# Output product of a gated feed-forward kernel: seven smaller products in place of a full product, taken product by product

## The chip, the cores and the metric

The kernel runs on one core of a Trainium2 chip. The metric is the device time of one execution in microseconds (us). A difference below about 0.3% cannot be told from no change here.

## The reference

Attention within chunks of 64 tokens, then a gated feed-forward layer over 4608 tokens with 512 features, all in fp32.

```python
# batch 8, heads 8, seq 576, head_dim 64, chunks of 64
scores = scale * (q_c @ k_c.T); attn = softmax(scores); out = attn @ v_c
x = out.transpose(0, 2, 1, 3).reshape(4608, 512)
xn = x / sqrt(mean(x * x, -1) + 1e-06) * rms_g
g = xn @ w_gate                       # w_gate, w_val: 512 x 1536
val = xn @ w_val
return (g * sigmoid(g) * val) @ w_out # w_out: 1536 x 512
```

## The kernel before

Every fp32 matrix is split into a high and a low part (`h`, `l`), and a product is three matmuls: high by high, high by low, low by high. All large matmuls have 128 columns of weights and 512 moving elements.

The tokens are nine tiles of 512 (`TT`). The first three tiles (tile zero, one, two; the loop `for t in range(PLAIN)`) take both layers as plain products: `gated` makes one 128-wide slice of the hidden features and `down` adds its share of the output to four PSUM banks `acc`. While tile zero runs, the weights are converted (`conv_step`); while tile one runs, the weights' sums for the gating products are made on GpSimd and stored to DRAM (`sides`, `save_plain`).

The last six tiles are three **blocks** of two tiles each (`for b in range(NB)`). In a block the gating product is taken in seven products instead of eight, by the scheme of Strassen and Winograd: tokens of the two tiles, and halves of the feature sums, are combined, and `product` takes one of the seven, P1 to P7, for one pair `i` of hidden slices (`up_pair`, six pairs per block). In each pair the order is P1, P5, P6, P2, P3, P7, P4 (`ORD`; the first pair has `FIRST`). One product is 12 matmuls into two banks, one for each `m` (gate and value part); `after` then collects the result with VectorE, ScalarE and GpSimd, in the tiles `p1`, `p5`, `u2`, `c11`, and writes the four parts of the gated result to `g[:, f, h]`, where `f` is the slice and `h` the tile: VectorE writes `g[:, 0, 0]` (L723), GpSimd `g[:, 0, 1]` after P3 (L740), `g[:, 1, 1]` after P7 (L734, behind two additions at L730) and `g[:, 1, 0]` after P4 (L746). I call this the **up phase**. Then comes the **down phase**: for each of the two tiles and each of the 12 slices `split_g` makes the high and the low part of `g` (ScalarE `gh` at L768, VectorE `gl` at L769, two buffers each), and `down` (L535) makes 12 matmuls with the weights `wo`, which `out_load` brings back from DRAM.

Beside both phases runs the attention of the next block's four **units** (of 256 tokens), one step after each product: `step()` counts the products, 42 in the up phase, and a table gives the steps. Unit n begins at step 4 + 10n, and `PAIR_STEPS` gives the distances of its seven parts: load (-4), `first` (0), `second` (3), `third` (5), `fourth` (8), and the two that turn the result (11, 13). `first` makes the scores on TensorE (`ps_s`, L239) in the two banks of the pool `ps_a`. `fourth` makes the values (`ps_o`, L361: 64 instructions, 128 in the trace) in the same two banks, and `turned_norm` empties each bank by one VectorE instruction (`xu<-ps_o`, L375). When the step counter is past 46, thus in the down phase, `x_sides` makes the next block's token sums and splits them (`xp`: ScalarE L614, VectorE L615; sums at L632; scaling by `rms_g` at L629), one piece per step.

TensorE follows the order of the code (`manual_schedule`); for VectorE, ScalarE, GpSimd and the DMA queue of SyncE a list scheduler sets the order when the program is built, and each engine then takes its instructions strictly in that order. Buffers are given by pools: `wts` has 18 tiles of 1 MB, which hold `g`, `xp`, and the loaded weights `wr` and `wo`.

## Time and profile before

| what | value |
|---|---|
| time, median of 3 runs | 937.97 us |
| lowest and highest of the 3 | 937.32 and 939.9 us |
| span of the profiled execution | 935.8 us |
| its own time | not among the three times; the median is 2.2 us over the span |
| TensorE matmul busy | 906.1 us, 97% of the span |
| VectorE busy | 516.8 us, 55% |
| ScalarE busy | 428.8 us, 46% |
| GpSimd busy | 173.3 us, 19% |

The span runs from the first to the last instruction. Busy time of TensorE counts overlapping matmuls once, and the mean duration of a single matmul in a list of groups is its latency; the pace is read from the chain of waits, where a run of matmuls has a length and a count.

### The profile page before, as it was taken

What the parts mean: (1) busy time and instruction counts of PE and PEld (TensorE: products, weight loads), DVE (VectorE), ACT (ScalarE), POOL (GpSimd) and SP (SyncE); (2) the same over time, 40 slices, a digit from 0 to 9 for tenths busy, and PEclk for the clock granted to TensorE, in tenths of its full rate; (3) what the DMA queues carried; (4) which work ended last, traced back from release to release, by engine and by line L of the source; (5) the groups of instructions that cost most, each with busy time, mean ns of one, the idle gap of its engine ahead of it and who ended that gap; (6) DMA issues with size and microseconds to landing.
All of it is one profiled execution on the core that took longest, in us unless ns stands there. A gap on an engine that the chain in (4) does not pass through costs nothing.

```text
span 935.8 us, 17332 instructions
## 1 busy us (share of the span) xinstructions
PE 906.1 (97%) x6936; PEld 742.1 (79%) x6936; DVE 516.8 (55%) x873; ACT 428.8 (46%) x695; POOL 173.3 (19%) x155
## 2 busy tenths in 40 slices
PE   4699999999999999999999999999999999999998
PEld 3478878888888788888888888888888888888886
DVE  5899983654556555754664735546656332333232
ACT  4989953453446543553444425445444223222222
POOL 0100012224200000233332002323330023224100
PEclk9999999999999999999999999999999999999999
DMA  9688998877975744767789666585986585337511
GB/s 344 241 317 313 342 324 325 264 255 235 304 272 157 188 153 145 274 213 279 252 293 341 271 272 260 208 299 180 331 321 260 237 331 209 135 135 298 241 46 46
DMA packets 78735, 231.82 MB, mean 248 GB/s; under 512 B 8384, under 2 KB 40128, under 8 KB 62912
## 3 DMA queue, kind: packets, MB, share of 16 engines
q1 hardware_dynamic: 78656, 230.72, 69.0%
q8 instruction: 55, 0.90, 0.4%
q14 instruction: 24, 0.20, 0.1%
HBM read 171.97 MB, written 58.72 MB: 247 GB/s over the span
## 4 chain that ended last, share of the span: by engine, by line
PE 83%; issue 5%; ACT 4%; DVE 3%; DMA 2%; POOL 1%; SPq 0%; ACTq 0%; POOLq 0%
PE acc L535 28%; PE ps_b L666 11%; PE ps_c L666 11%; PE ps_a L666 11%; PE ps_g L500 7%; PE ps_v L500 7%; PE ps_d L666 5%; PE ps_o L361 2%; PE ps_s L239 2%; ACT w L152 1%; POOL ri_u L465 1%; DMA x<-kT_dram 1%; DMA eT<-away_e 1%; ACT raw L153 1%; ACT e L279 1%
## 5 line engine op out<-in xcount | busy, mean ns | idle before, releaser
L535 PE MATMUL acc<-wo,gh 128*128 128x512 f32 x576 | 177.6, 390 | 0.0
L535 PEld LDWEIGHTS acc<-wo,gh 128*128 128x128 f32 x576 | 108.0, 188 | 22.5
L535 PE MATMUL acc<-wo,gl 128*128 128x512 f32 x288 | 112.3, 390 | 0.0
L769 DVE TENSOR_TENSOR gl<-g,gh 128x512 fp32r<-128x512 f32 x72 | 49.8, 691 | 101.2 <-ACT gh L768 99.2
L666 PE MATMUL ps_b<-xp,wr 128*128 128x512 f32 x432 | 104.6, 391 | 0.0
L666 PE MATMUL ps_c<-xp,wr 128*128 128x512 f32 x432 | 104.3, 390 | 0.0
L666 PE MATMUL ps_a<-xp,wr 128*128 128x512 f32 x432 | 103.5, 390 | 0.0
L500 PE MATMUL ps_g<-xh,parts 128*128 128x512 f32 x288 | 98.0, 400 | 4.4 <-ACT sg L518 3.7
L768 ACT CAST gh<-g 128x512 fp32r<-128x512 f32 x72 | 44.8, 623 | 116.1 <-PE acc L535 110.9
L500 PE MATMUL ps_v<-xh,parts 128*128 128x512 f32 x288 | 95.5, 391 | 0.0
L666 PEld LDWEIGHTS ps_a<-xp,wr 128*128 128x128 f32 x432 | 80.9, 188 | 16.9
L666 PEld LDWEIGHTS ps_c<-xp,wr 128*128 128x128 f32 x432 | 80.8, 188 | 16.9
L666 PEld LDWEIGHTS ps_b<-xp,wr 128*128 128x128 f32 x432 | 80.6, 188 | 17.1
L535 PE MATMUL acc<-parts,gh 128*128 128x512 f32 x288 | 90.3, 394 | 0.0
L740 POOL TENSOR_TENSOR g<-u,u 128x512 f32<-128x512 f32 x18 | 23.2, 1290 | 342.0 <-DVE u L736 244.4
L500 PEld LDWEIGHTS ps_g<-xh,parts 128*128 128x128 f32 x288 | 55.0, 191 | 17.9 <-ACT sg L518 4.6
L535 PEld LDWEIGHTS acc<-wo,gl 128*128 128x128 f32 x288 | 54.1, 188 | 11.8 <-DVE gl L769 0.5
L500 PEld LDWEIGHTS ps_v<-xh,parts 128*128 128x128 f32 x288 | 54.4, 189 | 11.3
L535 PEld LDWEIGHTS acc<-parts,gh 128*128 128x128 f32 x288 | 53.1, 188 | 11.4 <-ACT parts L177 0.2
L500 PE MATMUL ps_g<-xl,parts 128*128 128x512 f32 x144 | 57.0, 396 | 0.0
L535 PE MATMUL acc<-parts,gl 128*128 128x512 f32 x144 | 56.2, 391 | 0.0
L500 PE MATMUL ps_v<-xl,parts 128*128 128x512 f32 x144 | 56.2, 390 | 0.0
(111 smaller groups left out, 1356.1 us busy)
## 6 DMA issues: line engine op xcount, KB each, us to landing
wr<-wsd SPq DMA_DIRECT2D x63, 1024.0 KB, 7.4
wo<-wod SPq DMA_DIRECT2D x36, 1024.0 KB, 8.6
raw<-w_up_dram SPq DMA_DIRECT2D x12, 1024.0 KB, 8.6
vt<-v_dram SPq DMA_DIRECT2D x18, 512.0 KB, 7.0
wsd<-parts SPq DMA_DIRECT2D x18, 512.0 KB, 5.9
out_dram<-o SPq DMA_DIRECT2D x36, 256.0 KB, 2.2
qt<-qT_dram SPq DMA_DIRECT2D x17, 512.0 KB, 5.2
kt<-kT_dram SPq DMA_DIRECT2D x17, 512.0 KB, 6.1
```

What stands on the lines that cost most here:

```text
L152: nc.scalar.activation(w, high.bitcast(F32), AF.Abs, scale=2.0**16)
L153: nc.scalar.mul(low, low.bitcast(U32), 2.0**-29)
L239: nc.tensor.matmul(st["s"][j][c * CH : (c + 1) * CH, pr], st["q"][rows, pr, tok : tok + CH], st["k"][rows, pr, tok : tok + CH], start=True ...
L279: nc.scalar.activation(e[:, pr, j], st["s"][j][:, pr], AF.Exp, scale=SCALE, bias=mx[:, j, s, pr], accum_out=rs[:, s, pr, j],)
L361: nc.tensor.matmul(st["o"][(2 * c + t) * Q : (2 * c + t + 1) * Q, h * D : (h + 1) * D], eT[c][rows, t, h], vt[rows, c, h], start=True, sto ...
L465: nc.gpsimd.tensor_tensor(ri, ss, mhalf.broadcast_to([P, 2]), op=ALU.pow)
L500: nc.tensor.matmul(ps, a[f][:, cols], b[dt], start=(dt == 0 and i == 0), stop=(dt == NDT - 1 and i == 2),)
L535: nc.tensor.matmul(acc[s], a[:, cols], b, start=(f == 0 and i == 0), stop=(f == NF - 1 and i == 2),)
L666: nc.tensor.matmul(ps, w[:, a, m, cols], xp[:, b, kt], start=start and kt == 0 and i == 0, stop=stop and kt == 1 and i == 2, skip_group_ch ...
L740: nc.gpsimd.tensor_tensor(g[:, 0, 1], kp["u2"], kept[0]["u2"], op=mult)
L768: nc.scalar.copy(gh, src)
L769: nc.vector.tensor_tensor(gl, src, gh.bitcast(F32), op=ALU.subtract)
```

## The change

1. The output product of each block is taken in seven products too (`down_pair`). The four parts of `g` for one pair of slices are the left matrix's blocks; the weights' blocks are the halves of a pair of rows and the halves of the 512 output columns. The order is product by product, P1, P5, P2, P6, P3, P7, P4 (`DOWN`), and within a product the six pairs one after the other: 42 **groups** of six matmuls each. The weights are now the stationary side and the tokens the moving side, so the output comes out turned and is put in order on the host.
2. The sums of `g` are made on VectorE: two in the up phase, at the end of `up_pair` (a tile `tt` and one part of `g`), and two in the down phase, just after the split of P5 and of P6 has read `tt`.
3. The sums of the output weights are made while tile two runs: one joining addition and four smaller additions on GpSimd per pair, then four splits (ScalarE copy, VectorE difference) and four stores (`out_sides`). `save_plain` stores the plain parts in three DMAs per pair instead of one. The output weights come back in 11 loads per block instead of 12.
4. The attention units begin at steps 4, 12, 20 and 28 (`PAIR_AT`) instead of 4, 14, 24 and 34. Of `x_sides`, the scaling of the first two units stands at steps 29 and 30, the rest from step 45 on, every third step.

First place: TensorE in the up phase of the first block, from the product P3 of the second pair on. `ps_c` is P3, `ps_b` P7, `ps_o` the values of the first unit, `ps_d` P4, `ps_a` P1 of the next pair, `ps_s` the scores of the second unit. Before:

```order
L666 MATMUL ps_c<-xp,wr 128x512 x12
L666 MATMUL ps_b<-xp,wr 128x512 x12
L361 MATMUL ps_o<-vt,eT 32x64 x64
L666 MATMUL ps_d<-xp,wr 128x512 x12
L666 MATMUL ps_a<-xp,wr 128x512 x12
L239 MATMUL ps_s_4319<-kt,qt 64x64 x2
```

And in the changed kernel:

```order
L722 MATMUL ps_c<-xp,wr 128x512 x12
L722 MATMUL ps_b<-xp,wr 128x512 x12
L366 MATMUL ps_o<-vt,eT 32x64 x64
L244 MATMUL ps_s_4432<-kt,qt 64x64 x2
L244 MATMUL ps_s_4433<-kt,qt 64x64 x2
```

The scores of the second unit stood two products behind the values of the first; now they follow them at once, ahead of P4. Both use the two banks of `ps_a`. The same holds for the values of the second and the third unit, and in the second block.

Second place: VectorE at the same place. `u` is emptied after P3 and `p` after P7, `xu<-ps_o` empties the two banks of the values. Before:

```order
L736 TENSOR_TENSOR u_4128<-ps_c,u_4128 128x512
L736 TENSOR_TENSOR u_4130<-ps_c,u_4130 128x512
L729 TENSOR_TENSOR p_4074<-ps_b,p_4074 128x512
L729 TENSOR_TENSOR p_4076<-ps_b,p_4076 128x512
L375 TENSOR_TENSOR xu<-ps_o,rs 128x16x32 x2
```

And in the changed kernel:

```order
L797 TENSOR_TENSOR u_4288<-ps_c,u_4288 128x512
L761 TENSOR_TENSOR tt<-g 128x512
L790 TENSOR_TENSOR p_4226<-ps_b,p_4226 128x512
L790 TENSOR_TENSOR p_4228<-ps_b,p_4228 128x512
L762 TENSOR_TENSOR g<-g 128x512
L380 TENSOR_TENSOR xu<-ps_o,rs 128x16x32 x2
```

The two new sums of `g` stand ahead of the instructions that empty the banks: `tt` reads the part of `g` that GpSimd writes after P3, and `g<-g` the part that GpSimd writes after P7.

Third place: VectorE in the down phase of the first block, at the product P6 (six `gl<-tt`), in the changed kernel alone. `tt<-tt,g` are the sums after the split, `x2` and `t1` pieces of `x_sides`.

```order
L830 TENSOR_TENSOR gl_5696<-tt_4208,gh_5695 128x512
L676 TENSOR_SCALAR x2_2633<-x2_2633,g_col_98 128x8x64
L858 TENSOR_TENSOR tt_4208<-tt_4208,g_4026 128x512
L830 TENSOR_TENSOR gl_5715<-tt_4208,gh_5714 128x512
L679 TENSOR_TENSOR t1_5648<-x2_2633,t1_5648 128x1024
L830 TENSOR_TENSOR gl_5728<-tt_4208,gh_5727 128x512
L858 TENSOR_TENSOR tt_4208<-tt_4208,g_4211 128x512
L830 TENSOR_TENSOR gl_5741<-tt_4208,gh_5740 128x512
L858 TENSOR_TENSOR tt_4208<-tt_4208,g_4500 128x512
```

Between two differences `gl`, of which each group of six matmuls needs one, stands now about one further VectorE instruction.

The diff, cut to its core:

```diff
+PAIR_AT = 4, 12, 20, 28
+DOWN = P1, P5, P2, P6, P3, P7, P4
...
+    def out_sides(i, st):
...
+        def join():
+            w = st.tile([P, 2, DM], F32, tag="t1", bufs=1, name="wo")
+            raw = out_parts[i].bitcast(F32)
+            total(w, raw[:, 0], raw[:, 1], ALU.add)
...
+        def split():
+            for p, key in ((P7, (2, 1)), (P5, (2, 2)), (P6, (1, 1)), (P3, (1, 2))):
+                part = tmp.tile([P, 2, OH], F32R, tag="tmp", name="side")
+                nc.scalar.copy(part[:, 0], at[key])
+                nc.vector.tensor_tensor(
+                    part[:, 1], at[key], part[:, 0].bitcast(F32), op=ALU.subtract
+                )
+                nc.sync.dma_start(out_home(i, p), part.rearrange("p a c -> p (a c)").bitcast(F32))
...
-        nc.sync.dma_start(wod[i], flat(out_parts[i]).bitcast(F32))
+        raw = out_parts[i]
+        for p, f, half in ((P1, 0, 0), (P2, 1, 0), (P4, 1, 1)):
+            dst = out_home(i, p).rearrange("p (a c) -> p a c", a=2)
+            nc.sync.dma_start(dst, raw[:, :, f, half * OH : (half + 1) * OH].bitcast(F32))
...
-        return g
+        if i % PER == 0:
+            tt.append(big([P, PER, TT], F32, "tt"))
+        t = tt[-1][:, i % PER]
+        nc.vector.tensor_tensor(t, g[:, 0, 1], g[:, 0, 0], op=ALU.subtract)
+        nc.vector.tensor_tensor(g[:, 0, 1], g[:, 1, 1], g[:, 0, 1], op=ALU.subtract)
+        return g, t
...
+    def down_pair(t, gts, wos, step, more):
+
+        order = [(p, i) for p in DOWN for i in range(NPR)]
...
+            src = {
+                P1: g[:, 0, 0], P5: tt, P2: g[:, 1, 0], P6: tt,
+                P3: g[:, 1, 1], P7: g[:, 0, 1], P4: tt,
+            }[p]
+            ready[n] = split_g(src)
+            if p == P5:
+                nc.vector.tensor_tensor(tt, g[:, 1, 1], tt, op=sub)
+            elif p == P6:
+                nc.vector.tensor_tensor(tt, tt, g[:, 1, 0], op=sub)
...
+            split_next(n + 1)
+            gh, gl = ready.pop(n)
+            w = wos[n // PER][:, n % PER]
+            for k, (a, b) in enumerate(((0, gh), (1, gh), (0, gl))):
+                for m in range(2):
+                    nc.tensor.matmul(
+                        banks[m][name],
+                        w[:, a, m * P : (m + 1) * P],
+                        b,
...
+            if i == NPR - 1:
+                with urgent():
+                    finish(p, banks, kept)
+            step()
...
+            for i in range(NPR):
+                for k, f in enumerate(out_sides(i, st)):
+                    at.setdefault(3 * i + k, []).append(f)
...
-                    at.setdefault(4 + 10 * n + PAIR_STEPS[k], []).append(f)
+                    at.setdefault(PAIR_AT[n] + PAIR_STEPS[k], []).append(f)
+            first, both = x_sides(x, x2, st)
+            for n, f in enumerate(first):
+                at.setdefault(PAIR_AT[1] + PAIR_STEPS[-1] + 4 + n, []).append(f)
+            for n, f in enumerate(both):
+                at.setdefault(7 * NPR + 3 + 3 * n, []).append(f)
...
-                if step.n > 46 and made:
-                    made.pop(0)()
+        down_pair(t, gts, wos, step, b + 1 < NB)
```

`finish` collects the seven products as `after` does for the gating: ScalarE copies P1 and P5 out of their banks, VectorE adds the others, and the results are stored as they are ready.

## The prediction

> **What bounds the kernel now.** I read the page first, for the engines' shares.

> ```profile
> span 935.8 us, 17332 instructions
> PE 906.1 (97%) x6936; PEld 742.1 (79%) x6936; DVE 516.8 (55%) x873; ACT 428.8 (46%) x695; POOL 173.3 (19%) x155
> ```

> TensorE (PE) is nearly always busy. Whether it waits inside the blocks is seen in the chain of waits and in the busy time by stretches: up phase and down phase of the first block, then up phase of the last one.

> ```profile
> 497.64 62.97 PE acc L535 x276
> 560.61 5.44 PE ps_a L666 x24
> 866.37 65.29 PE acc L535 x288
> 931.66 0.02 issue
> ```

> ```profile
> 369.10:497.60 128.50, 128.50 (x1285) 105.34 (x1283) 80.27 (x149) 62.22 (x94) 41.71 (x36) 1.00 0.76 267
> 497.60:560.60 63.00, 63.00 (x280) 51.95 (x278) 33.88 (x45) 23.93 (x37) 1.10 (x2) 1.00 0.75 291
> 752.10:866.40 114.30, 114.30 (x506) 94.65 (x505) 38.08 (x56) 30.58 (x51) 36.80 (x29) 1.00 0.60 228
> ```

> The columns after the stretch are its length and the busy time of PE, weight loads, VectorE (DVE), ScalarE (ACT) and GpSimd (POOL). TensorE is busy for the whole of each stretch: nothing is waited for in the blocks, so each matmul less is worth its pace. The pace is 65.29 / 288 = 0.2267 us, so 12 matmuls take 2.72 us. VectorE is busy 80 of 128 us in the up phase and 34 of 63 us in the down phase; it has room, but work that is put in front of something TensorE needs has a price.

> **What is taken away.** The output products are these two groups of the page.

> ```profile
> L535 PE MATMUL acc<-wo,gh 128*128 128x512 f32 x576 | 177.6, 390 | 0.0
> L535 PE MATMUL acc<-wo,gl 128*128 128x512 f32 x288 | 112.3, 390 | 0.0
> ```

> They are 864 matmuls, 288 per block. Seven products of six pairs, three matmuls and two banks are 252. In three blocks 108 matmuls go: 108 x 0.2267 = 24.5 us, all on the path. The shape stays 128 columns by 512 elements, so the pace stays.

> **The scores behind the values (up phase).** This is the largest added term. After the change the scores of units two, three and four stand directly behind the values of the unit before, in the same two banks, and TensorE does not pass a waiting matmul by P4 or P1, which stand behind it. The banks come free when VectorE has run both instructions `xu<-ps_o`. In front of these, VectorE now has the two new sums of `g`, and they wait for GpSimd. The trace of before shows this very place, step 12 of the first block; only the scores aren't there.

> ```profile
> 402.86 2.88 PE L666 MATMUL ps_b<-xp,wr 128*128 128x512 f32 x12
> 403.06 0.69 DVE L736 TENSOR_TENSOR u<-ps_c,u 128x512 f32<-128x512 f32 x1 [0.67 <-PE ps_c L666]
> 403.90 1.29 POOL L740 TENSOR_TENSOR g<-u,u 128x512 f32<-128x512 f32 x1 [12.24 <-DVE u L736]
> 404.42 0.69 DVE L729 TENSOR_TENSOR p<-ps_b,p 128x512 f32<-128x512 f32 x1 [0.67 <-PE ps_b L666]
> 405.19 2.64 POOL L730 TENSOR_TENSOR p<-p,p 128x512 f32<-128x512 f32 x2
> 405.68 1.48 PE L361 MATMUL ps_o<-vt,eT 64*32 64x64 f32 x128
> 407.09 3.02 PE L666 MATMUL ps_d<-xp,wr 128*128 128x512 f32 x12
> 407.20 1.29 DVE L375 TENSOR_TENSOR xu<-ps_o,rs 128x512 f32<-128x512 f32 x2 [0.72 <-PE ps_o L361]
> 407.91 1.30 POOL L734 TENSOR_TENSOR g<-p,p 128x512 f32<-128x512 f32 x1
> ```

> I go through it with the new order. GpSimd ends the part of `g` after P3 at 405.19. Then VectorE makes `tt` (0.69, to 405.94) and only then the two `p<-ps_b,p` (to 406.67 and 407.36; before, the first began at 404.42). GpSimd's two additions end at about 408.05 and 409.37, its product (1.30) at 410.7. VectorE's second sum of `g` ends at 411.5, the two instructions that empty the banks (1.29) at 412.8. TensorE has issued the last of the values at 407.09 and goes on at 412.9: a wait of 5.8 us.

> At step 20 the values stand behind P4 instead of P7: TensorE is ready 2.72 later, and VectorE has one `p<-p,ps_d` (0.69) more in front: 413.6 - 409.8 = 3.8 us. At step 28 they stand behind P1 of the next pair, 5.44 later, and in front stand also four scalings by `rms_g` (0.51 each by the row below, 2.05): 415.6 - 412.5 = 3.1 us. Together 12.7 us per block, and the first and the second block have it: 25.4 us. The last block has no attention. From below the term is bounded by the bare emptying: 407.20 to 408.6 against 407.09, 1.5 us, six times: 9.0 us. From above I take 30, if softmax work of the units is also in front. Nothing can make it a gain, for before TensorE did not wait there.

> **VectorE in the down phase.** Durations are read from these groups.

> ```profile
> L769 DVE TENSOR_TENSOR gl<-g,gh 128x512 fp32r<-128x512 f32 x72 | 49.8, 691 | 101.2 <-ACT gh L768 99.2 <-PE acc L535 2.0
> L615 DVE TENSOR_TENSOR xp<-x,xp 128x1024 fp32r<-128x1024 f32 x15 | 18.1, 1215 | 1.9 <-ACT xp L614 1.7
> L632 DVE TENSOR_TENSOR t<-x,t 128x1024 f32<-128x1024 f32 x3 | 3.7, 1221 | 0.0
> L629 DVE TENSOR_SCALAR x<-x,g_col 128x512 f32<-128x512 f32 x24 | 11.2, 512 | 2.7 <-DMA x<-away_x 2.7
> ```

> TensorE needs 252 x 0.2267 = 57.1 us for the phase. VectorE gets 42 differences `gl`, 12 sums of `g` and 8 collecting additions, 62 x 0.69 = 42.8 us; in the first two blocks also seven `xp` (8.5), four sums (4.9) and four scalings (2.0): 58.2 us. It can't work ahead, since `gl` has two buffers, one of which TensorE reads. The difference for a group is free to start when the group two before it ends, and it is first read by the fifth of its group's six matmuls; with groups of 1.36 us that leaves 1.36 + 0.91 - 0.69 = 1.5 us of reserve. By the order, a product (8.16 us of TensorE) brings VectorE 8.8 us at P5, 8.8 at P2, 10.0 at P6 and 9.2 at P3: 4.2 us too much, less the reserve, 2.7 us. At the start, the last pair's second sum of `g` and `p<-p,ps_d` end 3.8 us after the phase begins (the same chain as above), so the third `gl` ends at 4.5 and is read at 3.6: 0.9 us. So 3.6 us in each of the first two blocks, where about a sixth is saved as instructions of one queue overlap (1.29 for two above), thus 3.0, and 0.9 in the last: 7 us. The bounds are 2 (only the starts) and 12 (the whole excess, and ScalarE's copies held up by it).

> **The clock.** One place of the trace shows what an idle TensorE brings after it.

> ```profile
> 130.71 0.50 PE L500 MATMUL ps_g<-xh,parts 128*128 128x512 f32 x1 [2.07 <-ACT sg L518]
> ```

> ```profile
> 130.71 4.55 PE ps_g L500 x12
> ```

> ```profile
> 130.00:135.00 5.00, 4.29 (x12) 3.40 (x13) 4.06 (x5) 3.10 (x6) 0.00 (x0) 0.69 1.01 324
> ```

> After 2.07 us without a matmul the granted clock falls to 0.69 in the next 5 us, and 12 matmuls take 4.55 instead of 2.72 us: 1.8 us lost. Each of the six waits above is longer than 2.07 us. Whether the clock falls must depend on where the gap lies, since the second of the two gaps of this kind (3.7 - 2.1 = 1.6 us by the row below) is no proof either way; I take four falls of 1.7, 6.8 us, between 0 and 6 x 1.8 = 11.

> ```profile
> PE ps_g L500 <- ACT sg L518: 3.7, 2, 2.1
> ```

> [...]

> **What is added beside the path.** In tile two, these rows are the nearest.

> ```profile
> 252.00:363.60 111.60, 110.14 (x1201) 89.99 (x1200) 58.53 (x123) 56.62 (x81) 4.33 (x8) 1.00 0.62 192
> ```

> ```profile
> L573 POOL TENSOR_TENSOR w<-w 128x512 f32<-128x512 f32 x24 | 32.5, 1354 | 79.4 <-DMA w<-wfd 40.3 <-DVE rs L323 26.9 <-DMA eT<-away_e 10.7
> L603 DVE TENSOR_TENSOR w<-w,side 128x512 fp32r<-128x512 f32 x24 | 17.4, 761 | 17.4 <-ACT side L601 13.3 <-DMA eT<-away_e 4.0
> L601 ACT CAST side<-w 128x512 fp32r<-128x512 f32 x24 | 13.6, 618 | 2.4 <-DVE gl L527 2.4
> ```

> GpSimd gets per pair 2.7 us for the join and about 2.7 for four sums of half the size: 33 us where it is busy 4. The 24 splits cost VectorE at most 18 us and ScalarE 15, in 111.6 us of which they use 59 and 57. TensorE's work hides that. The 24 stores stand in SyncE's queue among the attention's turns and hold the `tmp` buffers that `sg` of the gating needs too; a late store would stop the gating. I set 0.3, bounds 0 and 4. In tile one there are two DMAs more per pair and a quarter fewer bytes: nothing. The loads per block fall from 12 to 11.

> ```profile
> wo<-wod SPq DMA_DIRECT2D x36, 1024.0 KB, 8.6
> 411.64 1.25 DVE L389 STREAM_TRANSPOSE xu<-xu 128x1024 f32<-128x1024 f32 x1 [0.74 <-ACT xu L383]
> ```

> The first load of `wo` stands in SyncE's queue behind the turn of the fourth unit, which now falls at step 39. Its values start five products and 1.4 us before the down phase, 15 us; the turned result is there 412.9 - 405.7 = 7.2 us later, so the load is issued some 7.5 us ahead and lands in 8.6: 1 us late, with a bound of 0 and, for two blocks, 5. I set 1.0. At the end two VectorE additions stand behind the last matmul instead of one copy: 0.3. The up phase gets 12 sums more on VectorE (8.3 us to 80 of 128): away from the three steps these end long before TensorE comes back to the banks.

> **The sum.** 935.8 - 24.5 + 25.4 + 7.0 + 6.8 + 1.0 + 0.6 = 952.1 us of span. The profiled execution's own time isn't given; the median of the runs is 937.97 and thus 2.2 us over the span, which I keep: 954 us, slower by 1.7%. Below about 0.3% (2.8 us) a measurement can't tell a difference.

> **The rivals.**
> - Faster: the waits for the banks are only the bare emptying. In the trace, `xu<-ps_o` begins 0.1 us after the values end; it would stay so if GpSimd's products came earlier than I read. Then 935.8 - 24.5 + 9.0 + 2 + 1.6 = 924, with 2.2 about 926 us. Against it stands the order, in which both sums are in front of the emptying. It decides at 16 us of waits (24.5 - 7.0 - 1.6): with less, and no fall of the clock, the change gains. Chance 0.13.
> - No change: the waits are as worked out, but the clock holds and the down phase loses only its starts: 952.1 - 6.8 - 5 - 1.6 + 2.2 = 941; with waits of 23 instead of 25.4, 938. Chance 0.10.
> - Much slower: in the down phase ScalarE's casts of `xp` wait for VectorE's late sums, and the copies `gh` behind them are late too; each block then loses the full excess and the clock falls at all six waits: 952.1 + 5 + 4.6 + 2.2 = 964 us. Chance 0.12.
> - The forecast: 0.65.

> What is left out of the range is the faster case below 936 and the end of the slow one above 964. Faster by over 0.3% has 0.13, within 0.3% 0.10, slower 0.77.

> **What would show it.** Right: in the up phase of the first two blocks, three gaps on TensorE each in front of `ps_s`, of 5 to 6, about 4 and about 3 us, put down to VectorE's `xu`; granted clock under 1 there; none in the last block, whose length falls by 7 us. In the down phase VectorE busy about 58 of 60 us, and short waits of TensorE for `gl`. Wrong: `ps_s` following `ps_o` with gaps under 2 us; or the clock at 1.00 in the first block; or long waits in the last block's down phase, which would speak for a cause that I did not see.

## The result, and the profile after

The changed kernel takes 963.4 us (median of 4 runs, 959.86 to 964.65), the kernel before 937.64 (937.24 to 939.9). The ratio is 1.026, with a 95% interval of 1.0234 to 1.0285: slower. The forecast was 954 us, with a range of 936 to 964. The profiled execution took 964.65 us, the highest of the four; its span is 27.0 us longer than the one before.

The page of the changed kernel: span, and busy time of the engines.

```profile
span 962.8 us, 17569 instructions
PE 906.2 (94%) x6828; PEld 736.3 (76%) x6828; DVE 623.4 (65%) x1035; ACT 461.2 (48%) x771; POOL 218.6 (23%) x191
```

TensorE has 108 matmuls fewer and is busy for just as long, 906 us: some of its matmuls became slower. Busy time by stretches tells where. First the kernel before, cut where the phases begin: gating phase of the first three tiles, up and down phase of block one, down phase of the last block. Behind the length stand the busy times of PE, weight loads, DVE, ACT and POOL, then the granted clock.

```profile
37.45:368.90 331.45, 325.39 (x2736) 265.25 (x2737) 215.57 (x353) 190.47 (x319) 44.52 (x38) 0.99 0.77 257
368.90:493.34 124.44, 124.44 (x1145) 102.11 (x1144) 79.09 (x147) 61.33 (x93) 39.49 (x35) 1.00 0.75 262
493.34:560.44 67.10, 67.10 (x417) 55.22 (x416) 35.10 (x47) 24.82 (x39) 3.32 (x4) 1.00 0.77 298
866.20:931.65 65.45, 65.44 (x289) 53.87 (x287) 18.54 (x27) 15.65 (x26) 2.21 (x2) 1.00 0.25 101
```

The same view of the changed kernel: gating phase, then up and down phase of blocks one, two and three.

```profile
36.47:375.98 339.51, 328.60 (x2736) 266.19 (x2737) 229.56 (x377) 192.89 (x339) 78.80 (x68) 0.99 0.80 265
375.98:520.60 144.62, 134.34 (x1273) 110.34 (x1272) 90.09 (x163) 61.32 (x96) 39.69 (x36) 0.93 0.69 243
520.60:579.65 59.05, 58.54 (x253) 46.84 (x252) 54.02 (x76) 34.44 (x55) 7.05 (x5) 1.00 0.76 279
579.65:725.56 145.91, 135.22 (x1274) 111.00 (x1272) 82.46 (x156) 57.22 (x91) 39.71 (x36) 0.93 0.65 224
725.56:785.94 60.38, 59.31 (x253) 46.61 (x252) 54.19 (x76) 34.43 (x55) 7.01 (x5) 1.00 0.70 253
785.94:900.18 114.24, 114.24 (x505) 94.59 (x504) 44.93 (x68) 29.41 (x49) 34.99 (x28) 1.00 0.57 213
900.18:958.49 58.31, 57.86 (x253) 46.97 (x251) 42.26 (x62) 28.43 (x48) 7.05 (x5) 1.00 0.29 115
```

The down phase does what was planned: 7.1 us shorter in the last block. Up phase three is unchanged. Up phases one and two are 20 and 21 us longer than before (1.6 us of this is the fourth unit's values, which stood in the down phase), at a mean clock of 0.93: about 20 us of each ran at half clock (2 x 0.07 x 145). The gating phase, where hardly anything was expected, lost 8 us.

TensorE's waits: the row that carries the two up phases (sum, number, longest).

```profile
PE ps_s L244 <- DVE xu L380: 20.7, 12, 4.6
```

Twelve waits, two at each of the six places (one for each bank), 20.7 us. The timeline at the first place, step 12 of block one, with the idle time ahead of an instruction in brackets:

```profile
412.33 0.69 DVE L761 TENSOR_TENSOR tt<-g 128x512 f32<-128x512 f32 x1 [1.46 <-POOL g L801]
412.79 1.48 PE L366 MATMUL ps_o<-vt,eT 64*32 64x64 f32 x128
...
416.27 1.26 POOL L795 TENSOR_TENSOR g<-p,p 128x512 f32<-128x512 f32 x1
417.57 0.69 DVE L762 TENSOR_TENSOR g<-g 128x512 f32<-128x512 f32 x1 [3.35 <-POOL g L795]
418.18 1.28 DVE L380 TENSOR_TENSOR xu<-ps_o,rs 128x512 f32<-128x512 f32 x2
...
418.92 0.48 PE L244 MATMUL ps_s<-kt,qt 64*64 64x64 f32 x4 [4.65 <-DVE xu L380]
```

This is the chain that the prediction worked out: VectorE stands for 3.35 us in front of the second sum of `g`, until GpSimd's product is there; only then does it empty the bank, and TensorE begins the scores 4.65 us after the values. What follows it is in the chain of waits (start, length, number of matmuls),

```profile
419.61 1.97 PE ps_s L244 x60
421.58 4.20 PE ps_d L722 x12
425.77 2.72 PE ps_a L722 x12
```

and in the busy time of the stretch in which the clock is low here, and of one behind the wait at the third place:

```profile
417.38:424.21 6.83, 5.08 (x70) 4.25 (x71) 4.08 (x8) 2.73 (x6) 1.25 (x3) 0.50 0.23 68
478.94:485.80 6.86, 6.65 (x74) 5.49 (x75) 4.73 (x12) 4.01 (x8) 1.10 (x2) 0.51 0.47 190
```

For 6.83 us the clock is granted at half, at the first place from 1.5 us before the wait ends: 60 of the scores take 1.97 us, where the first unit's 64 take 1.09, and 12 matmuls take 4.20 in place of 2.72 us. The waits at the second and third place are 2.56 and 2.45 us long, and the fall behind them is as long as behind 4.65.

### The profile page after: what moved, and what is told of

It reads as the page before. It is cut to its first block, busy times and chain, and to the rows that moved or that the text cites. A ratio compares the mean times of both kernels' runs of the same rounds, so it can differ in the third digit from the quotient of the medians.

```text
span 962.8 us, 17569 instructions
## 1 busy us (share of the span) xinstructions
PE 906.2 (94%) x6828; PEld 736.3 (76%) x6828; DVE 623.4 (65%) x1035; ACT 461.2 (48%) x771; POOL 218.6 (23%) x191
## 4 chain that ended last, share of the span: by engine, by line
PE 58%; DVE 10%; issue 10%; ACT 7%; DMA 7%; POOL 6%; SPq 1%; DVEq 0%; POOLq 0%; ACTq 0%
PE ps_a L722 9%; PE ps_c L722 9%; PE ps_b L722 7%; PE ps_c L911 5%; PE ps_b L911 5%; PE ps_g L505 4%; PE acc L540 4%; PE ps_v L505 4%; PE ps_d L722 3%; PE ps_a L911 3%; POOL p L791 2%; PE ps_s L244 2%; DVE gl L830 1%; PE ps_d L911 1%; POOL g L795 1%
## 5 line engine op out<-in xcount | busy, mean ns | idle before, releaser
L722 PE MATMUL ps_c<-xp,wr 128*128 128x512 f32 x432 | 107.7, 400 | 0.0
L722 PE MATMUL ps_a<-xp,wr 128*128 128x512 f32 x432 | 107.1, 399 | 0.0
L722 PEld LDWEIGHTS ps_c<-xp,wr 128*128 128x128 f32 x432 | 83.6, 194 | 17.9
L722 PEld LDWEIGHTS ps_a<-xp,wr 128*128 128x128 f32 x432 | 83.5, 194 | 18.0
L769 ACT ACTIVATE p<-p 128x512 f32<-128x512 f32 x36 | 22.8, 633 | 85.2 <-POOL p L791 74.7
L830 DVE TENSOR_TENSOR gl<-g,gh 128x512 fp32r<-128x512 f32 x72 | 51.6, 732 | 12.3 <-ACT gh L829 10.9
L527 DVE TENSOR_TENSOR sg<-ps_v,sg 128x512 f32<-128x512 f32 x36 | 24.7, 686 | 51.5 <-PE ps_v L505 34.3
L722 PE MATMUL ps_d<-xp,wr 128*128 128x512 f32 x216 | 55.1, 406 | 0.0
L791 POOL TENSOR_TENSOR p<-p,p 128x512 f32<-128x512 f32 x36 | 45.8, 1291 | 25.4 <-DVE p L790 21.0
## 6 DMA issues: line engine op xcount, KB each, us to landing
wr<-wsd SPq DMA_DIRECT2D x63, 1024.0 KB, 6.5
wo<-osd SPq DMA_DIRECT2D x30, 1024.0 KB, 9.7
raw<-w_up_dram SPq DMA_DIRECT2D x12, 1024.0 KB, 8.4
```

The costliest lines, as they stand in the source:

```text
L527: nc.vector.tensor_tensor(sg, pv, sg, op=ALU.mult)
L722: nc.tensor.matmul(ps, w[:, a, m, cols], xp[:, b, kt], start=start and kt == 0 and i == 0, stop=stop and kt == 1 and i == 2, skip_group_ch ...
L769: nc.scalar.activation(t, t if src is None else src, AF.Silu)
L791: nc.gpsimd.tensor_tensor(kp["p5"], kp["p1"], kp["p5"], op=add)
L830: nc.vector.tensor_tensor(gl, src, gh.bitcast(F32), op=ALU.subtract)
```

## The experiments

Theory after this profile: the six waits for the banks and the half clock behind each are the loss in the blocks. The rivals: VectorE's load in the down phase, small matmuls as such lowering the clock, and the added work in the up phase. Each ratio is to the kernel before on the same chip. The stretches are the phases of the profiled execution, cut as above.

| run | us | ratio (95%) | gating | up 1 | down 1 | up 2 | down 2 |
|---|---|---|---|---|---|---|---|
| before | 937.6 | | 331.5 | 124.4 | 67.1 | 124.5 | 67.1 |
| changed | 963.4 | 1.026 (1.0234 to 1.0285) | 339.5 | 144.6 | 59.1 | 145.9 | 60.4 |
| spread | 943.6 | 1.0076 (1.0047 to 1.0105) | 339.8 | 125.2 | 68.0 | 126.1 | 70.0 |
| later | 943.4 | 1.0069 (1.0046 to 1.0091) | 341.6 | 134.7 | 59.1 | 131.2 | 60.4 |
| before_adj | 954.9 | 1.0192 (1.0165 to 1.0219) | 330.6 | 133.8 | 65.3 | 139.9 | 65.3 |
| pool_sums | 942.2 | 1.0065 (1.0038 to 1.0093) | 340.5 | 132.6 | 58.0 | 135.4 | 59.3 |
| fill | 959.7 | 1.0247 (1.0225 to 1.0268) | 340.1 | 142.1 | 59.1 | 141.5 | 60.3 |
| later_pool | 928.0 | 0.9912 (0.9888 to 0.9935) | 339.6 | 128.9 | 58.1 | 128.4 | 59.3 |
| raw_sides | 961.1 | 1.0271 (1.0242 to 1.0301) | 334.5 | 140.9 | 59.1 | 146.3 | 59.8 |
| later_pool_dve | 926.0 | 0.9885 (0.9846 to 0.9923) | 337.4 | 128.7 | 58.1 | 128.0 | 59.3 |
| later_pool_early | 928.8 | 0.9906 (0.9882 to 0.9931) | 340.0 | 128.3 | 58.1 | 128.4 | 59.6 |
| later_pool_dve_early | 928.4 | 0.9908 (0.9878 to 0.9938) | 337.1 | 127.8 | 58.2 | 128.2 | 59.3 |
| spread_ahead | 933.0 | 0.9966 (0.9948 to 0.9983) | 336.9 | 124.9 | 63.2 | 126.5 | 63.2 |
| plain_stores | 921.35 | 0.9843 (0.9817 to 0.987) | 329.7 | 129.6 | 58.1 | 129.0 | 59.3 |

An up phase with four units and no wait needs 126.1 us: up phase three (114.2) and what the units added before, (124.44 + 67.10) - (114.24 + 65.45) = 11.9 us.

**Spread: the scores away from the values.**

```diff
-PAIR_AT = 4, 12, 20, 28
+PAIR_AT = 4, 14, 24, 34
```

> The changed kernel with the attention units at steps 4, 14, 24 and 34 again, nothing else; scores no longer stand behind values. Theory (the waits of the scores for the two banks, and the halved clock behind each, make the loss): the three gaps of 4.6, 2.6 and 2.5 us per block go, the granted clock stays at 1.00 in both blocks, and the first two blocks come out about 7.6 us shorter than before, as the third one does; they lose 12.1 + 14.8 + 2 x 7.6 = 42 us against the changed kernel: about 921 us, at most 927 if the last unit, which now ends in the down phase, delays some differences there. Rival (VectorE's load in the down phase makes the loss): the last unit's work comes on top of it, TensorE waits there for gl, and the time stays at 940 to 960 us.

Measured: 943.6 us. The up phases came down to 125.2 and 126.1 at a clock of 1.00, as the theory says, but 921 us is missed by 22: the down phases grew by 9 us each. The waits of TensorE name the main cause, and it isn't the rival's.

```profile
PE ps_d L911 <- DMA wo<-osd: 8.1, 2, 4.5
PE ps_a L911 <- DVE gl L830: 2.0, 3, 0.8
PE ps_c L911 <- ACT gh L829: 1.7, 2, 0.8
```

The last load of the output weights now stands in SyncE's queue behind the stores of P7's results and comes 3.5 and 4.5 us late; the clock falls at both waits too (0.97 and 0.96 over the two phases). That the scheduler puts it elsewhere when units move was not in my reckoning.

**Spread_ahead: the same with that load earlier.**

```diff
-AHEAD_O = 3
+AHEAD_O = 4
```

> The kernel with units at steps 4, 14, 24 and 34 (spread), and the output weights loaded four ahead in place of three, so that the last load stands ahead of the stores of P7 in SyncE's queue and no longer behind them. Theory (the last load of wo, held by these stores, makes spread slow): the waits of 3.5 and 4.5 us in front of ps_d and the half clock behind them go, down phases from 68.0 and 70.0 to about 62 us, 943.6 - 13 = 931 us. Rival (the last unit's attention in the down phase overloads VectorE and ScalarE): the waits move to gl or gh, down phases stay at 66 us and more, 938 to 944 us.

Measured: 933.0 us, down phases of 63.2 us, no wait for `wo`. The theory's 931 is near. So about half of spread's miss was the load; 63.2 is still 4.4 us over the 57.1 for the matmuls and the 1.65 for the fourth unit's values. These 9 us in two blocks, of which the changed kernel has 5.2 as well, are at most the share of the rival.

**Later: the scores one product behind the values.**

```diff
-PAIR_STEPS = -4, 0, 3, 5, 8, 11, 13
+PAIR_STEPS = -4, 1, 3, 5, 8, 11, 13
```

> The changed kernel with the scores of each unit one product (2.72 us) later and all else in its place. Theory: the first gap of each block shrinks from 4.65 to about 1.9 us, the second and third from 2.5 to nothing. If the clock falls only after a wait of over 2 us, nothing is left of it: 963 - 42 + 4 = 925 us; if it falls after 1.9 us too, by 3.4 us each, 932 us. Rival (the clock falls because 64 small matmuls of values and 64 of scores stand close together, whatever the wait): the six falls stay, and the time is about 945 us.

Measured: 943.4 us. The waits shrank as expected,

```profile
PE ps_s L244 <- DVE xu L380: 2.4, 3, 1.8
PE ps_o L366 <- DMA eT<-away_e: 4.1, 6, 2.1
PE ps_s L244 <- issue: 2.3, 2, 1.3
```

from 20.7 to 2.4 us, and of the six falls of the clock one short one is left. ("Issue" stands for idle time in which the profile shows nothing that was waited for.) 31 to 38 us were to come back by the expectation, 20 did. The time alone would fit the rival's 945; that the falls are gone speaks against it. The up phases are still 13.7 us over 2 x 126.1: 2.4 are the waits for the banks, 1.7 the clock, 1.6 waits for `eT` in block one, 3.8 stalls in and behind the scores put down to issue, 0.4 short gaps; 3.7 us of longer busy time of TensorE I can't assign. The gating phase took 2 us more, 1.7 of them in tile zero, whose code this edit doesn't touch. And the 42 us that I reckoned with held too much: they let the down phases of the first two blocks fall to that of the third, which this edit doesn't touch.

**Before_adj: adjacency alone, in the kernel before.**

```diff
-                    at.setdefault(4 + 10 * n + PAIR_STEPS[k], []).append(f)
+                    at.setdefault((4, 12, 20, 28)[n] + PAIR_STEPS[k], []).append(f)
```

> The kernel before with only the attention units moved to steps 4, 12, 20 and 28; no sums of g, no new output product. Theory (adjacency costs at least the bare emptying of the banks): six waits of 1.4 to 1.6 us, 9 us together: 947 us if the clock holds over them, 957 us if each brings one stretch of 3.4 us at half clock (1.7 us lost). Rival (only the two sums in front of the emptying make TensorE wait): gaps under 0.5 us, 938 to 940 us.

Measured: 954.9 us, 18 more than before without a single sum of `g`.

```profile
PE ps_s L239 <- DVE xu L375: 6.9, 12, 0.8
PE ps_s L239 <- issue: 5.5, 3, 2.6
```

The waits for the banks are the bare emptying, about 1.15 us per place. At three of the six places the scores also stalled for 0.8 to 2.6 us with nothing that the profile shows to wait for. At just these three the clock fell, at the other three it stayed at 1.00; here are the second and the sixth place.

```profile
435.00:442.00 7.00, 6.51 (x86) 5.46 (x87) 4.89 (x14) 5.94 (x11) 1.25 (x3) 1.00 0.32 105
662.00:669.00 7.00, 3.64 (x68) 2.99 (x69) 3.87 (x10) 2.74 (x6) 1.10 (x2) 0.69 0.65 263
```

So the new spacing of the units costs 18 us by itself: its up phases lie 21.5 us over 2 x 126.1, those of the changed kernel 38.3.

**Pool_sums: the sums of `g` out of VectorE's queue.**

```diff
-        nc.vector.tensor_tensor(t, g[:, 0, 1], g[:, 0, 0], op=ALU.subtract)
-        nc.vector.tensor_tensor(g[:, 0, 1], g[:, 1, 1], g[:, 0, 1], op=ALU.subtract)
+        nc.gpsimd.tensor_tensor(t, g[:, 0, 1], g[:, 0, 0], op=ALU.subtract)
+        nc.gpsimd.tensor_tensor(g[:, 0, 1], g[:, 1, 1], g[:, 0, 1], op=ALU.subtract)
```

> The changed kernel with the two sums of g of the up phase on GpSimd in place of VectorE; the scores still stand directly behind the values. Theory (the sums lengthen the wait, the adjacency makes it): the gaps of a block shrink from 4.6, 2.6, 2.5 to about 1.4, 1.0 and 1.8 us, 12 us less in all: 951 us if the clock falls as before, 941 us if half of that goes, 931 us if it holds. Rival (the sums on VectorE don't matter, the emptying waits for something else): gaps and time within 3 us of the changed kernel's.

Measured: 942.2 us, the middle case. The waits fell from 20.7 to 8.1 us, and of the six falls of the clock one was left.

```profile
PE ps_s L244 <- DVE xu L380: 8.1, 12, 2.0
```

The sums in front of the emptying are thus what turned waits of 1.15 us into 2.45 to 4.65. Down phases also became 1 us shorter (59.1 to 58.0), which fits the late start that the prediction put down to the last pair's second sum.

**Fill: the waits kept, TensorE kept busy in them.**

```diff
+            if fill:
+                spare = bank(ps_acc, "spare")
+                w = xside[P1][:, 0, 0]
+                for _ in range(12):
+                    nc.tensor.matmul(
+                        spare, w[:, :P], w, start=True, stop=True, skip_group_check=True
+                    )
             sc = two_banks(ps_a, "ps_s")
```

> The changed kernel with 12 useless matmuls (128 columns by 512 elements, into a spare bank that nothing reads) between the values and the scores at each of the six places; 72 matmuls, 16.3 us of TensorE more. Theory (each wait costs itself and then 6.8 us at half clock, because TensorE idles in it): the waits of 4.65, 2.57 and 2.45 us become 1.9, 0 and 0, the clock holds, and the two up phases lose 16.3 + 4.5 us in place of 38.3 over what their matmuls need: 946 us; 949 us if the clock still falls for 3.4 us behind the two waits of 1.9 us. So 16 us of added work make the kernel 14 to 17 us faster. Rival (the clock falls with the small matmuls of values and scores, whether TensorE idles or not): the falls stay and the filling only replaces waiting, 963 + 16.3 - 15.5 = 964 us.

Measured: 959.7 us, and the interval meets that of the changed kernel: 16.3 us of useless matmuls more cost nothing. The time, between 949 and 964, decides nothing; the clock does. At four of the six places it is now 1.00, with values and scores as close as before but for the fill between them; here the first place of block one and the second:

```profile
420.00:427.00 7.00, 6.38 (x78) 5.23 (x79) 4.90 (x13) 5.21 (x9) 1.09 (x2) 0.76 0.28 84
447.00:454.00 7.00, 6.97 (x114) 5.49 (x99) 4.01 (x8) 3.44 (x8) 3.23 (x4) 1.00 0.28 116
```

So the small matmuls alone don't lower it, and the rival falls; the second place of before_adj above, where values and scores stand close together at a clock of 1.00, says the same. The theory's size, 946 us, was 14 us off: 4.8 us are stalls put down to issue (0.8, 1.6 and 2.3), 3.4 two short falls of the clock, for which it had allowed 949; the rest I can't assign.

**Later_pool: both cures,** the edits of later and of pool_sums.

```diff
+PAIR_STEPS = -4, 1, 3, 5, 8, 11, 13
...
+        nc.gpsimd.tensor_tensor(t, g[:, 0, 1], g[:, 0, 0], op=ALU.subtract)
+        nc.gpsimd.tensor_tensor(g[:, 0, 1], g[:, 1, 1], g[:, 0, 1], op=ALU.subtract)
```

> The changed kernel with both: the scores one product later, and the two sums of g of the up phase on GpSimd. Theory: no wait for the banks is left; the up phases fall from 132.6 and 135.4 us (sums on GpSimd alone) to about 126 each, the 114.2 of the last block and four units of attention: 942 - 16 = 926 us; 930 us if stalls of 1 to 1.5 us put down to nothing but issue remain inside the scores. Rival (the up phase is long because of the new work on VectorE and GpSimd, not of the banks): up phases of 131 us and more, 936 to 942 us.

Measured: 928.0 us, 0.9% faster than before (0.9888 to 0.9935). No wait for the banks is left, up phases are at 128.9 and 128.4, which leaves the rival (131 and more) out. The 2.5 us over 126.1 are about 1 us of issue stall in each block and small gaps.

**Raw_sides: tile two without GpSimd's sums.** In `out_sides`, `sums` does nothing and `join` names the high parts:

```diff
-            total(w, raw[:, 0], raw[:, 1], ALU.add)
...
-                    at[half + 1, f + 1] = w[:, f, half * OH : (half + 1) * OH]
+                    at[half + 1, f + 1] = raw[:, 0, f, half * OH : (half + 1) * OH]
```

> The changed kernel without GpSimd's 30 additions in tile two (the splits and stores then take the plain high parts, so the output weights' sums are left out of the computation). Theory (in tile two VectorE's instructions stand still while GpSimd adds, 6.34 us for four xl that took 2.7 before, and 2.6 us for a scaling of 0.5): the waits of 1.6 and 3.6 us and the half clock behind each go, the gating phase falls from 339.5 to about 332 us, 956 us in all. Rival (ScalarE's copies, VectorE's differences and the stores of the splits hold the buffers of sg): the gating phase stays at 337 to 340 us, 961 to 964 us.

The gating phase is 334.5 us, 5 of the 8 us won; in tile two alone it is 6.7 us (122.7 to 116.0). The times can't tell the kernels apart (1.0242 to 1.0301 against 1.0234 to 1.0285), and the 956 us of the theory are missed by 5. The profiled execution, 956.14 us, is the fastest of the four: in its first up phase, 140.9 us, one of the three waits brought no fall of the clock, with the same code there (see the last section). What went is seen in the group of the `xl`, first in the changed kernel, then here:

```profile
L480 DVE SCALAR_TENSOR_TENSOR xl<-x,g_col,xh 128x512 fp32r<-128x512 f32 x4 | 6.3, 1642 | 0.0
```

```profile
L480 DVE SCALAR_TENSOR_TENSOR xl<-x,g_col,xh 128x512 fp32r<-128x512 f32 x4 | 2.7, 743 | 0.0
```

In the changed kernel GpSimd's sums ran beside the `xl` of tile two, and TensorE waited for them:

```profile
252.32 2.38 POOL L578 TENSOR_TENSOR wo<-parts 128x1024 f32<-128x1024 f32 x1 [7.00 <-DMA wsd<-w]
252.32 6.34 DVE L480 SCALAR_TENSOR_TENSOR xl<-x,g_col,xh 128x512 fp32r<-128x512 f32 x4
254.78 4.47 POOL L578 TENSOR_TENSOR wo<-wo 128x256 f32<-128x256 f32 x4
255.30 0.50 PE L505 MATMUL ps_g<-xl,parts 128*128 128x512 f32 x1 [1.60 <-DVE xl L480]
```

**Later_pool_dve, later_pool_early, later_pool_dve_early: where to put the sums.** On later_pool, the first makes them on VectorE, the second moves them, the third does both.

```diff
-            nc.gpsimd.tensor_tensor(out, one, two, op=op)
+            nc.vector.tensor_tensor(out, one, two, op=op)
...
-                    at.setdefault(3 * i + k, []).append(f)
+                    at.setdefault(2 * i + k + 1, []).append(f)
```

> As later_pool, and in tile two the joining and the four sums of the output weights on VectorE in place of GpSimd (2.9 us per pair by the durations of xp and of side). Theory: VectorE no longer stands still there, the gating phase falls by about 8 us: 918 us, faster than the kernel before. Rival (17 us more of work in VectorE's queue delay sg of the gating just as much): no gain, 926 to 930 us.

> later_pool with the output weights' sums (on GpSimd) at two steps per pair from step 1 on in tile two, so that they end at step 13, ahead of the next tiles' token sums, and the first join no longer runs beside the four xl. Theory (the gating phase is 8 us longer because this work meets other work at two places: the join beside xl at the start, the last pair's sums beside the first token sums near the end): waits of 1.0 and 3.0 us go, the gating phase falls from 339.6 to 332 or 333 us, 921 us in all. Rival (it is the amount of work on VectorE and ScalarE, wherever it stands): new waits at earlier steps, gating phase 338 to 342 us, 926 to 930 us.

> The same order of steps with the sums on VectorE (later_pool_dve). Theory as for later_pool_early: gating phase from 337.4 to 332 or 333, 920 us. If GpSimd's use beside VectorE is what costs, this one is 2 to 4 us ahead of later_pool_early; if VectorE's queue is what costs, as much behind it.

All three miss: 926.0, 928.8 and 928.4 us, none to be told from 928.0. On VectorE the sums save 2 to 3 us of gating phase (337.4 and 337.1), since the four `xl` again take 2.7 us; moving them earlier saves nothing. In later_pool_early the scheduler left the first join beside the `xl` (5.7 us), and the wait of 3 us moved from the gating to the attention's values, behind a fetch that is late:

```profile
314.48 2.42 PE L366 MATMUL ps_o<-vt,eT 64*32 64x64 f32 x126 [3.86 <-DMA eT<-away_e]
```

So the rivals are nearer here: a wait removed at one step comes back at another.

**Plain_stores: the stores alone.** `join` and `sums` do nothing, and the stores copy the plain weights:

```diff
+            for p, f, half in ((P7, 0, 1), (P5, 1, 1), (P6, 0, 0), (P3, 1, 0)):
+                dst = out_home(i, p).rearrange("p (a c) -> p a c", a=2)
+                nc.sync.dma_start(dst, raw[:, :, f, half * OH : (half + 1) * OH].bitcast(F32))
```

> later_pool with the work of tile two cut down to its stores: GpSimd's sums, ScalarE's copies and VectorE's differences are left out, and the 24 stores take the plain output weights in their places (the weights' sums are left out of the computation). Theory A (the work on the three engines and the buffers that it holds lengthen tile two): gating phase from 339.6 to 331 or 332 us, 920 us. Theory B (the 24 stores in SyncE's queue hold up the attention's turns and loads): gating phase stays at 336 us or more, 924 to 928 us.

Measured: 921.35 us, gating phase 329.7 us at full clock.

```profile
37.68:367.40 329.72, 324.79 (x2736) 265.09 (x2737) 214.66 (x353) 190.58 (x319) 43.20 (x38) 1.00 0.83 273
```

That is theory A: the 24 stores in SyncE's queue cost nothing; the sums, copies and differences with the buffers they hold cost 9.9 us of the gating phase and 6.7 us of the time (928.0 to 921.35). Of the 9.9 us, 8.3 lie in tile two (119.4 to 111.1; 111.8 in the kernel before); the rest lies in tile zero and tile one, where the two kernels have the same code. Which of the copies, differences and buffers makes up what GpSimd's sums don't, the runs leave open. The changed kernel shows ScalarE standing twice, for 10.1 us, ahead of `sg` until a `side` is stored:

```profile
ACT L523 <- DMA osd<-side: 10.1, 2, 5.3
PE ps_g L505 <- ACT sg L523: 6.1, 3, 3.6
```

## Why the prediction was right or wrong

The sign and the place were right, and the time lies in the range, at its upper end. That it lies there is partly luck: the clock and tile two cost 18.6 us more than I set, each beyond its own upper bound, and the waits, the down phase, the first load and the ends 8.0 us less. The terms, beside what the profiled execution shows (27.0 us of span more):

| term | predicted | measured |
|---|---|---|
| 108 matmuls less | -24.5 | -24.5 |
| waits of the scores for the banks | 25.4 | 20.7 |
| the clock | 6.8 | 17.6 |
| VectorE in the down phase | 7.0 | 5.8 |
| tile two and the rest of the gating phase | 0.3 | 8.1 |
| first load of `wo` | 1.0 | 0 |
| the ends | 0.3 | -0.8 |

- **Matmuls: right.** 6936 matmuls became 6828; the last block's down phase shows it alone, 65.45 to 58.31 us with the late start of 1.0 in it.
- **Waits: the mechanism right, the size a fifth too large.** I forecast 5.8, 3.8 and 3.1 us; the first waits are 4.65, 2.56 and 2.45 us, each with some 0.2 more for the second bank. I let TensorE wait until both banks are empty, but the first scores need only the first one. Pool_sums shows that the sums are the longer part of the wait, before_adj what is left without them (6.9 us; my lower bound of 9.0 was too high for the same reason).
- **Clock: the step that failed most.** The up phases lost 38.3 us over their 126.1 each, and 20.7 are waits; 17.6 remain. Six rows of the chain, one behind each wait, bear most of it (12 matmuls in 4.20 to 4.86 us, 11.6 us more than 2.72 each), the 64 scores at half clock the rest. By the clock it comes out near that: at half clock TensorE was busy for 36.5 of the 41 us, and half of 36.5 is 18.3. I took four falls of 1.7 us, as the one in the trace before; there were six, each of 6.8 us in place of the 3.4 of that one, and each cost 2.9. My upper bound, 6 x 1.8, was made from this single row and was too low. This was the step to bound more widely: a price read from one event. That the fall depends on where the gap lies was right, and the traces show how (last section): the gap in the trace before, 2.07 us, lay inside one stretch of 3.41 us, and the clock was at half for one; at each of the six places TensorE was idle in the next stretch too, for 0.3 to 1.8 us, and the clock stayed at half for two.
- **VectorE in the down phase: right within a microsecond.** Over 252 x 0.2267 = 57.1 us the three phases have 1.9, 3.3 and 1.2 us, 6.3 in all, less 0.5 that was there before. Later_pool splits it: 58.1, 59.3 and 57.3 there, so that the late start accounts for 1.0 per block (0.9 forecast) and the token sums for 1 and 2 (3.0 forecast). VectorE is busy 54 of 59 us, not 58 of 60.
- **Tile two: wrong.** "TensorE's work hides that" was argued from busy shares (59 and 57 of 112 us). It asked whether there is room, not what stands in front of `sg` and `xl`. 1.6 and 3.6 us of waits came, and a short fall of the clock with each. My bound of 4 was too low, and by more than the 8.1 say: tile two is 10.9 us longer than before (111.8 to 122.7), and tile zero, whose code didn't change, 2.9 us shorter. Tile zero takes 113.0 to 116.4 us in the fourteen traces, so differences of a whole gating phase are known to some 3 us.
- **First load of `wo`: nothing there.** But spread shows 8.1 us of wait at the last load after a shift of the units, the sort of cost that I looked for at the wrong load.
- **The rivals.** 963.4 us is the time of "much slower". Its half about the clock came true, at more than the price it set; ScalarE's convoy in the down phase did not. The faster rival's condition, waits well below 16 us and a steady clock, is what later_pool makes, and it is 0.9% faster.

From 60 us on, every stretch at half clock before the last matmul is 3.41 or 6.83 us long in these traces, and TensorE did not always stand for the whole of the stretch ahead of it: waits of 2.45 us brought 6.83 us of half clock, and even with the wait of 4.65 us TensorE was busy for 0.30 of the 3.41 us ahead of the fall.

## What to carry to other kernels

A wait on TensorE can be paid twice here: in the changed kernel each wait of some 2.5 us cost itself and about 2.9 us of half clock, so count it as up to 5. In these traces the fall followed every time where 1.84 us or more of idle time lay in one stretch of 3.41 us (34 of 34), and the stretches lay differently in each trace. Before an instruction is put behind another that shares its buffers, list what the emptying engine has queued in front, above all work that waits for a third engine; one product of distance and another engine for two sums turned 2.6% slower into 0.9% faster. Work that is "beside the path" needs the same look, at the queue and at its buffers, and not a sum of busy shares.

## What the runs showed of the hardware

```profile
444.69:448.10 3.41, 1.53 (x129) 1.32 (x128) 1.51 (x4) 0.83 (x2) 2.04 (x2) 1.00 0.56 233
448.10:454.93 6.83, 5.94 (x72) 4.91 (x73) 4.73 (x13) 3.32 (x7) 2.36 (x3) 0.50 0.18 68
```

```profile
439.82:443.23 3.41, 1.69 (x130) 1.32 (x128) 1.50 (x3) 0.97 (x2) 2.19 (x2) 1.00 0.68 281
443.23:446.65 3.42, 2.22 (x68) 1.92 (x69) 1.69 (x5) 2.40 (x6) 2.37 (x3) 1.00 0.01 2
446.65:453.48 6.83, 6.83 (x32) 5.65 (x31) 6.05 (x15) 5.66 (x9) 0.00 (x0) 1.00 0.61 223
```

  In tile zero of pool_sums a wait of 3.07 us, cut into 1.32 and 1.75, brought no fall; in tile two of the changed kernel one of 1.60 us brought one. Of the 39 falls, none had a second stretch at half where TensorE stood for 0.16 us or less of the first (21 falls); where it stood for 0.29 us or more, 17 of 18 had one. The stretches lie differently against the first instruction in each trace: counted from it they begin at 2.15 us and multiples of 3.413 us more in the kernel before, at 0.95 in the changed one. What the small matmuls count for in this, no run shows.
- **VectorE beside GpSimd.** Four `xl` took 6.34 us while GpSimd added, and 2.7 us without (before, raw_sides and later_pool_dve). Near the end of tile two one scaling, 0.48 us at the median of the 24, took 2.62 us and ended 0.3 us after the join; `xp` behind it came late, and `sg` behind that:

```profile
333.79 3.32 POOL L578 TENSOR_TENSOR wo<-parts 128x1024 f32<-128x1024 f32 x1 [9.54 <-DVE side L598]
334.76 2.62 DVE L676 TENSOR_SCALAR x<-x,g_col 128x512 f32<-128x512 f32 x1
```

  What holds VectorE up at these two places, no run shows.
- **Stalls put down to issue.** With scores close behind other small matmuls or the fill, TensorE stood for 0.8 to 2.6 us inside the scores at some places, with nothing in the trace that it waited for. The kernel before has none. The cause is open.
